# A pre-norm linear-attention and token-mixing block: the attention numerator computed for two token tiles at a time, with the order of the work around it rewritten

## The chip, the cores and the metric

The program runs on one core of a Trainium2 chip, in one launch, with all inputs and the output in the chip's main memory. The metric is device microseconds (us) of one execution, lower is better. Engines are named as the profile names them: PE (matrix multiplication), PEld (its weight loads), DVE (vector engine), ACT (activation engine), POOL (GpSimd) and SP (which only issues transfers here).

## The reference, cut to what matters

The input x has 2048 tokens and 512 channels. There are 32 heads of 16 channels, and the hidden width of the token mixer is 1792.

```python
def _A_ref(x, wqkv, w_phi, wo):
    q, k, v = heads(x @ wqkv)
    pq = jnp.einsum("bhsd,hdf->bhsf", q, w_phi)
    pk = jnp.einsum("bhsd,hdf->bhsf", k, w_phi)
    phi_q = jnp.concatenate([_softmax(pq), _softmax(-pq)], axis=-1)
    phi_k = jnp.concatenate([_softmax(pk), _softmax(-pk)], axis=-1)
    kv = jnp.einsum("bhsf,bhsd->bhfd", phi_k, v)
    z  = jnp.einsum("bhsf->bhf", phi_k)
    num = jnp.einsum("bhqf,bhfd->bhqd", phi_q, kv)
    den = jnp.einsum("bhqf,bhf->bhq", phi_q, z)[..., None] + 1e-6
    return merge(num / den) @ wo

def _B_ref(x, w1, b1, w2, b2):
    h = _layernorm(x)
    u = _gelu(jnp.einsum("bsd,sf->bdf", h, w1) + b1)
    return transpose(jnp.einsum("bdf,fs->bds", u, w2) + b2)

h = x + _A_ref(_layernorm(x), A_wqkv, A_w_phi, A_wo)
h2 = h + _B_ref(_layernorm(h), B_w1, B_b1, B_w2, B_b2)
```

Everything is float32. Two products that need float32 accuracy at speed are split: an operand is written as a high part and a low remainder in a shorter format (`F32R`), and three matmuls (high×high, high×low, low×high) take the place of one. `mm3` issues such a triple, `split` makes the two parts: ACT copies the high part, another engine subtracts it from the source.

## The kernel before

The tokens are cut into 16 tiles of 128. The program has four stages. First the weights are folded and k, v of all tiles are computed, which gives the summed matrix kv and the sums z. Six tiles' q logits are made in that stage too. The second stage, a loop `for it in range(NT + 3)`, is where the change lies: it finishes attention tile by tile, adds the residual, normalizes, and begins the token mixer. The third stage does the rest of the mixer's first matrix, the fourth its second matrix.

In the second stage a token tile t goes through these steps:

- `q_mm` (12 matmuls, PE) makes the q logits, `logit_ops` (three passes on DVE, from tile 6 on a fourth and fifth on POOL, in `negate`) subtracts the maximum and minimum, `exps` (ACT) takes the exponential into the tile `eq`, and `q_sum` (two reductions on DVE) makes the softmax sums.
- `s_ez` (POOL, line 442) multiplies `eq` with z; `s_den` (six small DVE operations) makes from it the weights `w` that hold both softmax sums and the denominator; `s_pq` (POOL, line 460) multiplies `eq` with `w`.
- `s_tr` transposes the eight blocks of `eq` on PE (line 525) into the PSUM tile `tn`, and ACT copies it to `pht` (line 527, two copies).
- `s_num` multiplies with kv: 16 small matmuls (line 543), each on 64 rows and 32 columns of the array, with 128 moving columns, into `tn` again. ACT copies the high part to `oh` (line 547), DVE the rest to `ol` (`s_ol`, line 552).
- `s_wo` (12 matmuls, PE) multiplies with the output weights into the PSUM tile `po`; `s_h` (DVE, line 568) adds x and sends the sum h to the output; SP issues that transfer.
- `s_moments` (ACT), `s_rstd` (two tiny POOL operations, lines 579 and 580) and `s_hn` normalize h: `hn` and the high part of `hs` on ACT (lines 584 and 57), the low part of `hs` on POOL (line 58).
- `fill(p)` then adds this tile's share to hidden column pair p of the mixer's first matrix (6 matmuls, PE). Its weights come by `fill_load`: a transfer on SP, the high part on ACT (line 604), the low part `wlo` on DVE (line 596), which is put off until `flush`.

The order on PE, DVE, ACT and POOL in this stage is the order of the program's text (`manual_schedule`); each engine works off its list strictly in order. Only SP's list, and all lists from the third stage on, are set by a planner. A tile's buffer is written again when its last reader is done: `tn` and `po` have one buffer, `pht`, `oh` and `ol` two, `h` four.

An iteration `it` works on different tiles at once: `s_num(it-1)`, `s_wo(it-2)`, `s_tr(it)`, `s_pq(it+1)`, `s_den(it+2)`, `s_ez(it+3)`, `s_moments`, `s_rstd` and `s_hn` of `it-3`, `fill(0)` for tile `it-4`, and, once all q logits are done, up to two steps of `fill(1)`. On PE an iteration is thus: 16 numerator matmuls, 12 for wo, 8 transposes, 12 for a q tile or two fills. On POOL it is: `s_pq`, `s_rstd`, `s_ez`, as long as there are any the two operations of `negate`, and the low part of `hs`.

Of the kernel before, what the change touches and what calls it, by code (L numbers as in the profile page):

```python
# [9 lines left out]
F32 = mybir.dt.float32  # L10
F32R = mybir.dt.float32r
# [13 lines left out]
Q_AT = (4, 6, 8, 9, 11, 13)  # L25
V_NOT = (0, 1, 11)
SUMS = 8
LAG = 4
WARM = 9
EPS = 1e-5  # L30

# [2 lines left out]
def block_kernel(ctx: ExitStack, tc: tile.TileContext, x, xT, wT, phic, wo, w1, b1, w2, b2,  # L34
# [25 lines left out]
    def mm3(o, ah, al, bh, bl, first, last):  # L60

        nc.tensor.matmul(o, ah, bh, start=first, stop=False)  # L62
        nc.tensor.matmul(o, ah, bl, start=False, stop=False)  # L63
        nc.tensor.matmul(o, al, bh, start=False, stop=last)  # L64
# [90 lines left out]
    def negate():  # L155

        if MN:
            ev, mx, mn = MN.pop(0)
            nc.gpsimd.tensor_sub(mn, mn, mx)
            nc.gpsimd.tensor_sub(ev[:, :, 1], mn.unsqueeze(3).to_broadcast([P, NPR, 2, DH]), ev[:, :, 0])  # L160

    def turns(*lists):

        return [ops[i] for i in range(max(map(len, lists))) for ops in lists if i < len(ops)]

    def run(*lists):
        for op in turns(*lists):
            op()
# [197 lines left out]
    def q_logits(lag):  # L366
        n = q["logits"]
        if n < min(NT, q["mm"] - lag + NT * (q["mm"] == NT)):
            EQ[n] = big.tile([P, NG, P], F32, name="eq", tag="big")
            q["logits"] += 1  # L370
            return logit_ops(PS[n], EQ[n], n >= len(Q_AT))
        return []
# [7 lines left out]
    def q_sums(lag):  # L380
        n = q["sum"]
        if n < min(NT, q["exp"] - lag + NT * (q["exp"] == NT)):
            q["sum"] += 1
            return q_sum(n)
        return []
# [54 lines left out]
    def s_ez(t):  # L440
        EZ[t] = az.tile([P, NG, P], F32, name="ez")
        nc.gpsimd.tensor_mul(EZ[t], EQ[t], zB)  # L442

    def s_den(t):


        tz = az.tile([P, NPR, 2, 2], F32, name="tz")
        den = az.tile([P, NPR, 2], F32, name="den")
        W[t] = az.tile([P, NPR, 2, 2], F32, name="w", bufs=3)
        other = SQ[t]  # L450
        return [lambda: nc.vector.reduce_sum(tz.rearrange("p g c h -> p (g c h)"), heads(EZ[t]), axis=AX.X),
                lambda: nc.vector.scalar_tensor_tensor(tz[:, :, 0], other[:, :, 1], 1e-6, tz[:, :, 0],
                                                       op0=ALU.mult, op1=ALU.add),
                lambda: nc.vector.tensor_mul(tz, other, tz),
                lambda: nc.vector.reduce_sum(den, tz.rearrange("p g c h -> p g h c"), axis=AX.X),
                lambda: nc.vector.reciprocal(den, den),
                lambda: nc.vector.tensor_mul(W[t], other, den.unsqueeze(2).to_broadcast([P, NPR, 2, 2]))]  # L457

    def s_pq(t):
        nc.gpsimd.tensor_mul(heads(EQ[t]), heads(EQ[t]), W[t].rearrange("p g c h -> p (g c h)").unsqueeze(2).to_broadcast([P, 2 * H, DH]))  # L460

    def lead(it, mm):

        if 0 <= it + 3 < NT:
            s_ez(it + 3)
        negate()
        for _ in range(mm):
            q_mm()
        q_exp(0)
# [49 lines left out]
    HN, HT, PHT, OS, PO, VE = {}, {}, {}, {}, {}, {}  # L519

    def s_tr(t):
        PHT[t] = ak.tile([P, NG, P], F32, name="pht")
        ptr = ps_t.tile([P, 2, 4, P], F32, name="tn")
        for g in range(NG):
            nc.tensor.transpose(ptr[:, g // 4, g % 4, :], EQ[t][:, g, :], ident)  # L525
        for half in range(2):
            nc.scalar.activation(PHT[t][:, half * 4:half * 4 + 4, :], ptr[:, half], AF.Copy)  # L527

    def s_kv():

        pt = ps_o.tile([P, 2, P], F32, name="po")
        for b in range(2):
            nc.tensor.transpose(pt[:, b, :], kvS[:, 2 * b:2 * b + 2, :].rearrange("p n f -> p (n f)"), ident)
        nc.scalar.activation(kvB, pt, AF.Copy)

    def s_num(t):

        pn = ps_t.tile([P, 2, 4, P], F32, name="tn")[:, :, 0:2]
        for b in range(2):
            for c in range(4):  # L540
                for r in range(2):
                    rows, cols = slice(64 * r, 64 * r + 64), slice(32 * c, 32 * c + 32)
                    nc.tensor.matmul(pn[cols, r, b, :], kvB[rows, b, cols], PHT[t][rows, 4 * b + c, :],  # L543
                                     start=True, stop=True, skip_group_check=True)
        oh = ak.tile([P, 2, 2, P], F32R, name="oh")
        ol = ak.tile([P, 2, 2, P], F32R, name="ol")
        nc.scalar.activation(oh, pn, AF.Copy)
        OS[t] = oh, ol, pn

    def s_ol(t):  # L550
        oh, ol, pn = OS[t]
        return [lambda: nc.vector.tensor_sub(ol, pn, oh)]

    def s_wo(t):
        oh, ol, _ = OS.pop(t)
        PO[t] = po = ps_o.tile([P, D], F32, name="po")
        for j in range(4):
            mm3(po, oh[:, j // 2, j % 2, :], ol[:, j // 2, j % 2, :], woh[:, j, :], wol[:, j, :], j == 0, j == 3)

    def s_x(t):  # L560
        HT[t] = ak.tile([P, D], F32, name="h", bufs=4)
        nc.sync.dma_start(HT[t], x[t * P:(t + 1) * P, :])

    def s_h(t):

        h = HT[t]
        VE[t] = ak.tile([P, 4], F32, name="ve2", bufs=3)
        nc.vector.scalar_tensor_tensor(h, PO.pop(t), 1.0, h, op0=ALU.mult, op1=ALU.add, accum_out=VE[t][:, 2:3])
        nc.sync.dma_start(out[t * P:(t + 1) * P, :], h)

    def s_moments(t):

        junk = ak.tile([P, D], F32, name="hj", bufs=1)
        nc.scalar.activation(VE[t][:, 1:2], VE[t][:, 2:3], AF.Copy, scale=-1.0 / D)
        nc.scalar.activation(junk, HT[t], AF.Square, bias=VE[t][:, 1:2], accum_out=VE[t][:, 3:4])
        nc.scalar.activation(VE[t][:, 0:1], VE[t][:, 3:4], AF.Identity, scale=(1.0 + EPS) / D, bias=eps2)
# [5 lines left out]
    def s_hn(t):  # L582
        hn = ak.tile([P, D], F32, name="hn")
        nc.scalar.activation(hn, HT[t], AF.Identity, scale=r2[:, t:t + 1], bias=VE[t][:, 1:2])
        HN[t] = big.tile([P, 2, D], F32R, name="hs", tag="big")
        split(HN[t][:, 0], HN[t][:, 1], hn, nc.gpsimd)
# [6 lines left out]
    def flush():  # L593
        while LATER:
            wl_, raw, wh_ = LATER.pop(0)
            LO.append(nc.vector.tensor_sub(wl_, raw, wh_).ins)  # L596
# [14 lines left out]
    def fill_load(p):  # L611
        if FL[p] < NT:
            WI[p, FL[p]] = stream(w1v, FL[p], 2, p * 256, 256)
            FL[p] += 2

    def fill(p, pool=None):

        t = FN[p]
        FN[p] = t + 1
        if FL[p] <= t:  # L620
            fill_load(p)
            flush()
        if t == 0:
            PU[p] = [pool.tile([P, D], F32, name="pu", tag="pu") for _ in range(2)]
        a, b = WI[p, t - t % 2]
        for c in range(2):
            mm3(PU[p][c], a[:, t % 2, c * P:(c + 1) * P], b[:, t % 2, c * P:(c + 1) * P],
                HN[t][:, 0], HN[t][:, 1], t == 0, t == NT - 1)

    for it in range(NT + 3):  # L630
        if 0 <= it < NT:
            s_x(it)
        if 0 <= it - 1 < NT:
            s_num(it - 1)
        if 0 <= it - 3 < NT:
            s_moments(it - 3)
        if 0 <= it - 2 < NT:
            s_wo(it - 2)
        if it == 1:
            run(q_logits(0))  # L640
            q_mm()
        if 0 <= it < NT:
            s_tr(it)
        if it == 0:
            s_kv()
        if 0 <= it + 1 < NT:
            s_pq(it + 1)
        if 0 <= it - 3 < NT:
            s_rstd(it - 3)
        lead(it, 1)  # L650
        den = s_den(it + 2) if it + 2 < NT else []
        ql = q_logits(1)
        ops = turns((s_ol(it - 1) if 0 <= it - 1 < NT else []) + ql + (q_sums(0) if it > 0 else []), den)

        at = 7 if ql else 3
        ops[at:at] = [flush]
        ops[3:3] = [lambda: s_h(it - 2)] if 0 <= it - 2 < NT else []
        run(ops)
        if it > 0:
            negate()  # L660
        if 0 <= it - 3 < NT:
            s_hn(it - 3)
        if FN[0] <= it - LAG:
            fill(0, ps_f)
        for _ in range(2):
            if q["logits"] == NT and FN[1] <= it - LAG:
                fill(1, ps_q)
        for p in range(2):
            if it >= LAG - 2 and FL[p] <= FN[p] + 1:
                fill_load(p)  # L670
    flush()
    ms.close()
# [197 lines left out]
```

## Time and profile before

| | us |
|---|---|
| median of 3 runs (532.62 to 533.29) | 532.62 |
| the profiled execution | 532.78 |
| its span in the profile | 531.0 |
| PE busy | 522.6 (98%) |
| DVE busy | 379.0 (71%) |
| ACT busy | 272.2 (51%) |
| POOL busy | 231.0 (44%) |
| granted PE clock | 1.00 |

The second stage lies from about 144 to 268 us of the span. A share of busy time is a mean over the whole span: POOL has little to do from 268 us on, and much before. The profile's list of the chain shows work that followed without a gap, so there the start of a piece to the start of the next is the time that it costs on the path; the duration of a single PE matmul in the other views is longer than that, since matmuls overlap. A releaser in a row (`<-`) is what ended an engine's idle time before it.

### The profile page before, as it was taken

What the parts mean: (1) busy time and instruction counts of PE and PEld (TensorE: products, weight loads), DVE (VectorE), ACT (ScalarE), POOL (GpSimd) and SP (SyncE); (2) the same over time, 40 slices, a digit from 0 to 9 for tenths busy, and PEclk for the clock granted to TensorE, in tenths of its full rate; (3) what the DMA queues carried; (4) which work ended last, traced back from release to release, by engine and by line L of the source; (5) the groups of instructions that cost most, each with busy time, mean ns of one, the idle gap of its engine ahead of it and who ended that gap; (6) DMA issues with size and microseconds to landing.
All of it is one profiled execution on the core that took longest, in us unless ns stands there. A gap on an engine that the chain in (4) does not pass through costs nothing.

```text
span 531.0 us, 9886 instructions
## 1 busy us (share of the span) xinstructions
PE 522.6 (98%) x3872; PEld 450.6 (85%) x3872; DVE 379.0 (71%) x680; ACT 272.2 (51%) x460; POOL 231.0 (44%) x190
## 2 busy tenths in 40 slices
PE   8999999999999999999999999999999999999995
PEld 7888888886877877777888888888899999999995
DVE  6993999877699888774426424735668878888874
ACT  6998833524237667766657323526444243343340
POOL 2589699877979988985335000000001101100110
PEclk9999999999999999999999999999999999999999
DMA  8633310012302233333255333542015556536641
GB/s 312 193 123 119 90 32 21 1 45 96 101 2 93 68 98 120 120 120 109 91 172 166 102 97 99 160 119 81 20 41 111 135 151 155 124 120 144 136 78 43
DMA packets 45487, 55.85 MB, mean 105 GB/s; under 512 B 3968, under 2 KB 33024, under 8 KB 45440
## 3 DMA queue, kind: packets, MB, share of 16 engines
q1 hardware_dynamic: 43136, 51.38, 31.0%
q0 software_dynamic: 2016, 3.67, 5.4%
q8 instruction: 30, 0.49, 0.4%
q10 hardware_dynamic: 288, 0.17, 0.1%
q14 instruction: 17, 0.14, 0.1%
HBM read 46.81 MB, written 8.39 MB: 104 GB/s over the span
## 4 chain that ended last, share of the span: by engine, by line
PE 93%; DVE 4%; ACT 1%; issue 1%; POOL 0%; DVEq 0%; ACTq 0%; POOLq 0%
PE py L764 26%; PE pu L62 12%; PE pu L64 12%; PE pu L63 12%; PE po L62 3%; PE po L63 3%; PE po L64 3%; PE tn L525 3%; PE pv L63 2%; PE pv L64 2%; PE pv L62 2%; PE pk_ps L62 2%; PE pk_ps L64 2%; PE pk_ps L63 2%; PE tn L543 2%; PE kvp L207 1%
## 5 line engine op out<-in xcount | busy, mean ns | idle before, releaser
L802 POOL DMA_DIRECT2D out<-ot x14 | 12.5, 999 | 211.7 <-DVE ot L800 211.7
L764 PE MATMUL py<-uf,whi 128*128 128x256 f32 x560 | 96.2, 283 | 0.0
L57 ACT ACTIVATE whi<-wraw 128x1792 fp32r<-128x1792 f32 x28 | 47.7, 1705 | 77.9 <-PE py L764 67.2
L62 PE MATMUL pu<-hs,whi 128*128 128x512 f32 x224 | 87.6, 394 | 0.0
L63 PE MATMUL pu<-hs,whi 128*128 128x512 f32 x224 | 87.3, 390 | 0.0
L64 PE MATMUL pu<-hs,wlo 128*128 128x512 f32 x224 | 87.1, 390 | 0.2 <-DVE wlo L596 0.2
L764 PEld LDWEIGHTS py<-uf,whi 128*128 128x128 f32 x560 | 83.3, 192 | 0.0
L596 DVE TENSOR_TENSOR wlo<-wraw,whi 128x512 fp32r<-128x512 f32 x56 | 45.1, 816 | 48.2 <-ACT whi L604 47.8
L764 PE MATMUL py<-uf,wlo 128*128 128x256 f32 x280 | 70.0, 283 | 0.0
L58 DVE TENSOR_TENSOR wlo<-wraw,whi 128x1792 fp32r<-128x1792 f32 x28 | 56.6, 2023 | 18.1 <-ACT whi L57 18.0
L604 ACT ACTIVATE whi<-wraw 128x512 fp32r<-128x512 f32 x56 | 34.4, 626 | 45.5 <-PE pu L63 41.4
L64 PEld LDWEIGHTS pu<-hs,wlo 128*128 128x128 f32 x224 | 42.1, 188 | 9.3 <-DVE wlo L596 0.6
L764 PEld LDWEIGHTS py<-uf,wlo 128*128 128x128 f32 x280 | 49.7, 192 | 0.0
L63 PEld LDWEIGHTS pu<-hs,whi 128*128 128x128 f32 x224 | 42.1, 188 | 8.4
L62 PEld LDWEIGHTS pu<-hs,whi 128*128 128x128 f32 x224 | 42.1, 188 | 8.4
L442 POOL TENSOR_TENSOR ez<-eq,zB 128x1024 f32<-128x1024 f32 x16 | 39.1, 2446 | 2.5 <-ACT zB L488 2.5
L764 PE MATMUL py<-un,whi 128*128 128x256 f32 x224 | 38.4, 283 | 0.0
L195 POOL TENSOR_TENSOR pk<-pk,sk 128x1024 f32<-128x1024 f32 x16 | 31.0, 1940 | 9.8 <-DVE sk L194 9.0
L527 ACT ACTIVATE pht<-tn 128x512 f32<-128x512 f32 x32 | 17.4, 595 | 34.5 <-PE tn L525 34.5
L460 POOL TENSOR_TENSOR eq<-eq,w 128x1024 f32<-128x1024 f32 x16 | 31.0, 1940 | 5.4 <-DVE w L457 5.4
L764 PEld LDWEIGHTS py<-un,whi 128*128 128x128 f32 x224 | 33.2, 192 | 0.1
L199 POOL TENSOR_TENSOR zacc<-zacc,pk 128x1024 f32<-128x1024 f32 x13 | 31.2, 2404 | 0.6
(165 smaller groups left out, 1187.6 us busy)
## 6 DMA issues: line engine op xcount, KB each, us to landing
wraw<-in_w SPq DMA_DIRECT2D x112, 256.0 KB, 3.0
xraw<-in_xT SPq DMA_DIRECT2D x16, 256.0 KB, 3.0
xh<-in_x SPq DMA_DIRECT2D x16, 256.0 KB, 2.6
h<-in_x SPq DMA_DIRECT2D x16, 256.0 KB, 3.6
out<-h SPq DMA_DIRECT2D x16, 256.0 KB, 2.0
out<-ot POOLq DMA_DIRECT2D x14, 256.0 KB, 4.4
wraw<-in_wT SPq DMA_DIRECT2D x12, 256.0 KB, 5.0
wo<-in_wo SPq DMA_DIRECT2D x4, 256.0 KB, 4.2
```

What stands on the lines that cost most here:

```text
L57: nc.scalar.activation(hi, src, AF.Copy)
L58: lo_engine.tensor_sub(lo, src, hi)
L62: nc.tensor.matmul(o, ah, bh, start=first, stop=False)
L63: nc.tensor.matmul(o, ah, bl, start=False, stop=False)
L64: nc.tensor.matmul(o, al, bh, start=False, stop=last)
L195: nc.gpsimd.tensor_mul(heads(PK[t]), heads(PK[t]), sk.unsqueeze(2).to_broadcast([P, 2 * H, DH]))
L199: nc.gpsimd.tensor_add(zacc, zacc, PK[t])
L442: nc.gpsimd.tensor_mul(EZ[t], EQ[t], zB)
L460: nc.gpsimd.tensor_mul(heads(EQ[t]), heads(EQ[t]), W[t].rearrange("p g c h -> p (g c h)").unsqueeze(2).to_broadcast([P, 2 * H, DH]))
L596: LO.append(nc.vector.tensor_sub(wl_, raw, wh_).ins)
L604: nc.scalar.activation(wh_, raw, AF.Copy)
L764: nc.tensor.matmul(o, a[x], b[:, y], start=start and i == 0, stop=stop and i == 2, skip_group_check=True)
```

## The change

`s_num` takes a pair of token tiles: `pht` holds both tiles' transposes side by side, and each of the 16 small matmuls has 256 moving columns, filling all of `tn`. It is called in even iterations only, so there are 8 calls in place of 16. `oh` and `ol` hold a pair, still made by one ACT copy and one DVE subtraction for each token tile. `pht`, `oh` and `ol` now have one buffer, of twice the size.

The loop's body has a new order. On PE an even iteration is: numerator of the pair, the q tile's 12 matmuls or the fills, wo, transposes; an odd one: q tile or fills, transposes, wo. `fills` puts both fills in one place, `fill(0)` for tile `it-5` (`LAG` is 5) and `fill(1)` one tile behind it. On DVE the subtractions `ol` of the pair come first, with the first step of `s_den` between them, and `s_h` comes last, behind `flush`. On POOL an even iteration is now `s_pq(it+1)`, low part of `hs` for tile it−4, `s_ez(it+3)`, `s_rstd(it-3)`, low part of `hs` for tile it−3; an odd one is `s_pq`, `s_ez`, `s_rstd`, with `negate`'s operations behind as before. On ACT an even iteration is: the two copies `oh`, `s_hn(it-4)`, the exponential, `s_moments(it-3)`, the copies of `pht`, `s_hn(it-3)`, the weights' high part; an odd one: the exponential, copies of `pht`, `s_moments(it-3)`, the weights' high part. `fill` flushes only if its own weights are still waiting, and `fill_load` runs by a new condition.

```diff
-LAG = 4
+LAG = 5
...
     def s_tr(t):
-        PHT[t] = ak.tile([P, NG, P], F32, name="pht")
+        j, i = divmod(t, 2)
+        if i == 0:
+            PHT[j] = ak.tile([P, NG, 2, P], F32, name="pht", bufs=1)
...
-    def s_num(t):
-
-        pn = ps_t.tile([P, 2, 4, P], F32, name="tn")[:, :, 0:2]
+    def s_num(j):
+
+
+        pn = ps_t.tile([P, 2, 4, P], F32, name="tn")
...
-                    nc.tensor.matmul(pn[cols, r, b, :], kvB[rows, b, cols], PHT[t][rows, 4 * b + c, :],
+                    nc.tensor.matmul(pn[cols, r, 2 * b:2 * b + 2, :], kvB[rows, b, cols], PHT[j][rows, 4 * b + c, :, :],
...
+        oh = ak.tile([P, 2, 2, 2, P], F32R, name="oh", bufs=1)
+        ol = ak.tile([P, 2, 2, 2, P], F32R, name="ol", bufs=1)
+        pv = pn.rearrange("p r (b i) s -> p i r b s", i=2)
+        for i in range(2):
+            nc.scalar.activation(oh[:, i], pv[:, i], AF.Copy)
...
+    def fills(it):
+        if FN[0] <= it - LAG:
+            fill(0, ps_f)
+        if FN[1] < it - LAG:
+            fill(1, ps_q)
+
     for it in range(NT + 3):
...
+        even = it % 2 == 0
+        if 0 <= it + 1 < NT:
+            s_pq(it + 1)
...
+        if it > 1 and even:
+            if it <= NT:
+                s_num(it // 2 - 1)
+            if it >= 4:
+                s_hn(it - 4)
+        den = s_den(it + 2) if it + 2 < NT else []
+        if it > 1 and even and it <= NT:
+            ol = s_ol(it // 2 - 1)
+            run(ol[:1] + den[:1] + ol[1:])
+            den = den[1:]
+        if it < NT:
+            s_x(it)
+        if it + 3 < NT:
+            s_ez(it + 3)
+        negate()
+        q_mm()
+        fills(it)
+        q_exp(0)
+        logits = q_logits(1)
+        if it >= 3 and even:
+            s_moments(it - 3)
+        if it > 1 and even and it - 2 < NT:
+            s_wo(it - 2)
+        if 1 < it < NT:
+            s_tr(it)
+        if it > 1 and not even and it - 2 < NT:
+            s_wo(it - 2)
+        if it >= 3 and not even:
+            s_moments(it - 3)
+        if it >= 3:
+            s_rstd(it - 3)
+        run(logits + (q_sums(0) if it > 0 else []), den)
+        flush()
+        if 0 <= it - 2 < NT:
+            s_h(it - 2)
+        if it > 0:
+            negate()
+        if it >= 3 and even:
+            s_hn(it - 3)
         for p in range(2):
-            if it >= LAG - 2 and FL[p] <= FN[p] + 1:
+            if it >= LAG - 3 + p and FL[p] <= FN[p] + 2 * (FN[p] > 0):
                 fill_load(p)
```

More of the change, by code (lines that the diff above doesn't have):

```diff
@@ L526, in s_tr @@
         for half in range(2):
-            nc.scalar.activation(PHT[t][:, half * 4:half * 4 + 4, :], ptr[:, half], AF.Copy)
+            nc.scalar.activation(PHT[j][:, half * 4:half * 4 + 4, i, :], ptr[:, half], AF.Copy)
     def s_kv():
@@ L542, in s_num, with s_ol @@
                     rows, cols = slice(64 * r, 64 * r + 64), slice(32 * c, 32 * c + 32)
-                    nc.tensor.matmul(pn[cols, r, b, :], kvB[rows, b, cols], PHT[t][rows, 4 * b + c, :],
+                    nc.tensor.matmul(pn[cols, r, 2 * b:2 * b + 2, :], kvB[rows, b, cols], PHT[j][rows, 4 * b + c, :, :],
                                      start=True, stop=True, skip_group_check=True)
[L545 to L552, printed above, removed]
+        oh = ak.tile([P, 2, 2, 2, P], F32R, name="oh", bufs=1)
[3 more added lines that the diff above has]
+            nc.scalar.activation(oh[:, i], pv[:, i], AF.Copy)
+        OS[j] = oh, ol, pv
+    def s_ol(j):
+        oh, ol, pv = OS[j]
+        return [lambda i=i: nc.vector.tensor_sub(ol[:, i], pv[:, i], oh[:, i]) for i in range(2)]
     def s_wo(t):
-        oh, ol, _ = OS.pop(t)
+        oh, ol, _ = OS[t // 2]
+        i = t % 2
         PO[t] = po = ps_o.tile([P, D], F32, name="po")
         for j in range(4):
-            mm3(po, oh[:, j // 2, j % 2, :], ol[:, j // 2, j % 2, :], woh[:, j, :], wol[:, j, :], j == 0, j == 3)
+            mm3(po, oh[:, i, j // 2, j % 2, :], ol[:, i, j // 2, j % 2, :], woh[:, j, :], wol[:, j, :], j == 0, j == 3)
     def s_x(t):
@@ L621, in fill @@
             fill_load(p)
+        if any(part is WI[p, t - t % 2][1] for part, _, _ in LATER):
             flush()
@@ L628, in fill @@
                 HN[t][:, 0], HN[t][:, 1], t == 0, t == NT - 1)
-    for it in range(NT + 3):
[L631 to L638, printed above, removed]
+    def fills(it):
[3 more added lines that the diff above has]
+            fill(1, ps_q)
+    for it in range(NT + 3):
+        even = it % 2 == 0
+        if 0 <= it + 1 < NT:
+            s_pq(it + 1)
+        if it == 0:
+            s_tr(0)
+            s_kv()
         if it == 1:
@@ L641, in block_kernel @@
             q_mm()
-        if 0 <= it < NT:
-            s_tr(it)
[L644 to L648, printed above, removed]
-            s_rstd(it - 3)
[L650 to L658, printed above, removed]
+            s_tr(1)
+        if it > 1 and even:
[22 more added lines that the diff above has]
+        if 1 < it < NT:
+            s_tr(it)
+        if it > 1 and not even and it - 2 < NT:
[3 more added lines that the diff above has]
+        if it >= 3:
+            s_rstd(it - 3)
+        run(logits + (q_sums(0) if it > 0 else []), den)
+        flush()
+        if 0 <= it - 2 < NT:
+            s_h(it - 2)
         if it > 0:
             negate()
-        if 0 <= it - 3 < NT:
+        if it >= 3 and even:
             s_hn(it - 3)
[L663 to L667, printed above, removed]
         for p in range(2):
-            if it >= LAG - 2 and FL[p] <= FN[p] + 1:
+            if it >= LAG - 3 + p and FL[p] <= FN[p] + 2 * (FN[p] > 0):
                 fill_load(p)
```

## The prediction

> **What bounds the kernel now.** I read the page's busy line first, then the chain, then the second stage by iterations.
>
> ```profile
> PE 522.6 (98%) x3872; PEld 450.6 (85%) x3872; DVE 379.0 (71%) x680; ACT 272.2 (51%) x460; POOL 231.0 (44%) x190
> ...
> POOL 2589699877979988985335000000001101100110
> ```
>
> PE is busy 98% of the span and so is the bound, but POOL's mean of 44% hides a stretch: slices 11 to 18, which hold most of the second stage, are at 8 or 9 tenths. One row per iteration (columns: stretch, length, busy time of PE, PEld, DVE, ACT, POOL, then clock, DMA share, GB/s) shows how near POOL is there.
>
> ```profile
> 181.38:189.00 7.62, 7.62 (x68) 6.10 (x66) 6.38 (x15) 5.78 (x11) 7.46 (x7) 1.00 0.34 105
> 189.00:197.56 8.56, 8.35 (x70) 6.27 (x70) 7.28 (x13) 6.18 (x12) 6.32 (x7) 1.00 0.27 92
> ...
> 211.97:219.13 7.16, 7.16 (x67) 5.67 (x65) 6.05 (x14) 4.21 (x9) 7.08 (x6) 1.00 0.46 149
> ```
>
> An iteration takes 7.16 us, all of it PE, and POOL is busy for 7.08 of them. So PE sets the pace, with POOL a hair behind. The chain of waits has these pieces of an iteration (start, length on the path, what), and the stage's one visible stall:
>
> ```profile
> 177.84 0.60 PE tn L543 x32
> ...
> 190.70 2.06 DVE wlo L596
> 192.80 0.50 PE pu L64
> ...
> 211.97 0.88 PE tn L525 x8
> 215.58 0.60 PE tn L543 x32
> 216.18 0.43 PE po L62
> 216.61 0.23 PE po L63
> ...
> 219.13 0.87 PE tn L525 x8
> ```
>
> The rows 181.38 to 197.56 hold two iterations (14.32) and one fill more (6 matmuls at 0.23, 1.38): 15.70 against 16.18, so that stall costs 0.5.
>
> **The numerator itself.** A burst of 16 small matmuls (32 records, two passes each) costs 0.60 until the next matmul starts, and that one 0.43 instead of 0.23, so 0.20 for changing over. What would 256 columns cost?
>
> ```profile
> L543 PE MATMUL tn<-pht,kvB 64*32 64x128 f32 x512 | 10.7, 275 | 0.0
> L207 PE MATMUL kvp<-pk,vs 128*32 128x64 f32 x512 | 9.1, 221 | 0.0
> ```
>
> 64 columns more lengthen a record by 54 ns, 0.84 ns a column. Eight places of the array (2 row halves, 4 column strips) work side by side, so 32 records are 4 in a row: 4 × 128 × 0.84 = 0.43 us, and 0.17 to fill and drain. A pair's burst is then 4 × 256 × 0.84 + 0.17 = 1.03, against 2 × 0.60, and changes over once: 0.17 + 0.20 = 0.37 saved a pair, eight pairs 3.0. Ends: 0.60 a burst if only the number of records counted (0.80 a pair, 6.4), and nothing saved (0). I take 3.0, since it follows from two rows.
>
> The Trainium skill, "TensorE: Matmul & The Clock Gate", section "Wait — 56ns, not 53.3ns?", says that matmuls never start closer than about 25 ns. By it 32 records would need 0.80 us, a pair would save 0.57 + 0.20, and eight pairs 6.2, 3.2 more. The trace has 32 records in 0.60, 19 ns each, so I don't use the rule.
>
> PE needs 2 × 7.16 − 0.37 = 13.95 a pair of iterations if nothing waits.
>
> **What moves at no cost.**
>
> ```profile
> L547 ACT ACTIVATE oh<-tn 128x512 fp32r<-128x512 f32 x16 | 9.5, 596 | 7.2 <-PE tn L543 7.2
> L552 DVE TENSOR_TENSOR ol<-tn,oh 128x512 fp32r<-128x512 f32 x16 | 11.0, 689 | 23.1 <-ACT oh L547 23.1
> ...
> wraw<-in_w SPq DMA_DIRECT2D x112, 256.0 KB, 3.0
> h<-in_x SPq DMA_DIRECT2D x16, 256.0 KB, 3.6
> ```
>
> ACT and DVE have as many `oh`, `ol` and `pht` operations as before. After a burst ACT and DVE need 0.60 + 0.69 until the first `ol` is there, while a q tile or fills (12 × 0.23 = 2.8) now lie between; without them wo would wait 1.5. The transposes wait for the second `ol`, another 2.8 later. `h` at DVE's end is wanted by the next wo (one `po` buffer), over 2 us on. SP has the same transfers (x in, h out, one weight block an iteration), which land in 3.0 to 3.6 us within a 7 us iteration. With fills later, one more is left after the last wo (7 for 6); PE's work is the same. Tile 15's `hs` must then be ready: h, moments, rstd, hn, hs and two weight copies are about 7 us by my estimate, and 44 matmuls (10 us) stand before its first use. All 0, at most 1 at that end.
>
> **POOL's ring.** Here I find the price. POOL's list in one iteration, from start to start:
>
> ```profile
> 162.74 1.94 POOL L460 TENSOR_TENSOR eq<-eq,w 128x1024 f32<-128x1024 f32 x1
> ...
> 176.47 0.25 POOL L159 TENSOR_TENSOR mn<-mn,mx 128x32 f32<-128x32 f32 x1
> 176.80 1.06 POOL L160 TENSOR_TENSOR eq<-mn,eq 128x512 f32<-128x512 f32 x1
> 177.82 1.28 POOL L58 TENSOR_TENSOR hs<-hn,hs 128x512 fp32r<-128x512 f32 x1
> ...
> 203.92 1.94 POOL L460 TENSOR_TENSOR eq<-eq,w 128x1024 f32<-128x1024 f32 x1 [0.59 <-DVE w L457]
> 205.82 0.55 POOL L579 TENSOR_TENSOR r<-ve,mhalf 128x1 f32<-128x1 f32 x1
> 206.45 0.19 POOL L580 TENSOR_TENSOR ve<-ve,r 128x1 f32<-128x1 f32 x1
> 206.59 2.40 POOL L442 TENSOR_TENSOR ez<-eq,zB 128x1024 f32<-128x1024 f32 x1
> 208.95 1.29 POOL L58 TENSOR_TENSOR hs<-hn,hs 128x512 fp32r<-128x512 f32 x1
> 210.20 1.93 POOL L460 TENSOR_TENSOR eq<-eq,w 128x1024 f32<-128x1024 f32 x1
> ```
>
> So pq 1.90, rstd 0.77, ez 2.36, hs 1.25 (and negate 1.35 while q logits are made): 6.28 an iteration, 12.56 a pair. In the order before, ez stands between rstd and hs and covers the normalizing on ACT. In the even iteration after, hs of tile it−3 follows its rstd directly. That wait, and the two ACT jobs behind it, look like this where POOL had nothing else to do:
>
> ```profile
> 261.78 0.19 POOL L580 TENSOR_TENSOR ve<-ve,r 128x1 f32<-128x1 f32 x1
> 262.00 0.82 ACT L584 ACTIVATE hn<-h,ve,r 128x512 f32<-128x512 f32 x1 [0.93 <-POOL ve L580]
> 262.85 0.63 ACT L57 ACTIVATE hs<-hn 128x512 fp32r<-128x512 f32 x1
> 263.56 1.29 POOL L58 TENSOR_TENSOR hs<-hn,hs 128x512 fp32r<-128x512 f32 x1 [1.59 <-ACT hs L57]
> ...
> 255.81 1.08 ACT L527 ACTIVATE pht<-tn 128x512 f32<-128x512 f32 x2 [1.89 <-PE tn L525]
> 263.39 1.14 ACT L604 ACTIVATE whi<-wraw 128x512 fp32r<-128x512 f32 x2
> ```
>
> POOL idles 1.6: 14.2 a pair. And POOL and DVE shut each other out when DVE subtracts `wlo`:
>
> ```profile
> 198.29 2.41 POOL L442 TENSOR_TENSOR ez<-eq,zB 128x1024 f32<-128x1024 f32 x1
> 198.78 3.07 DVE L596 TENSOR_TENSOR wlo<-wraw,whi 128x512 fp32r<-128x512 f32 x2
> ...
> 212.72 0.72 POOL L580 TENSOR_TENSOR ve<-ve,r 128x1 f32<-128x1 f32 x1
> 213.39 2.85 POOL L442 TENSOR_TENSOR ez<-eq,zB 128x1024 f32<-128x1024 f32 x1
> ...
> 212.69 1.29 DVE L596 TENSOR_TENSOR wlo<-wraw,whi 128x512 fp32r<-128x512 f32 x2
> ```
>
> Two wlo that meet an ez last 3.07 in place of 1.29, ending 0.6 a piece after it; two that come first lengthen ve and ez by 0.53 and 0.45. So 0.5 of POOL's time for each, two a pair. By DVE's new order the even one is issued just behind its w, while POOL is in ez, the odd one while POOL is in pq; neither falls into the 1.6 of idling. The ring rstd, ACT's hn and hs, POOL's hs, pq, ez, rstd, pq, hs, ez, rstd is then 14.2 + 1.0 = 15.2, 1.25 above PE's 13.95. PE feels it because ACT copies the odd tile's `pht` behind that hn and hs, and the next numerator waits for the copies.
>
> The Trainium skill, "SBUF — State Buffer", section "Who interferes with whom", says that a DVE operation with two SBUF inputs and a GpSimd operation that reads SBUF exclude each other for the whole instruction; by the full wlo (0.60) the ring would be 15.4 and the sum below 0.6 higher. The rows above give 0.5.
>
> **When it begins and ends.** pq of tile 4 starts at 162.74 in the trace before, set by DVE, which has much the same list in front of it after. From there POOL must do, up to the ez of tile 9: 4 pq (7.6), 4 ez (9.4), 3 rstd (2.3), 3 negate (4.1), 3 hs (3.8), two wlo (0.9) and about 1 of waits: 29.1, until 191.8. Then rstd 0.8 and the hand-over 1.6, hs at 194.2; ACT's two weight copies (1.1) and the copies of `pht` (1.1) let the pair numerator of iteration 8 start at 196.4. PE without waits: the burst at 177.84 has the same work behind it as two PE pieces (transposes 0.87, wo 2.75) before iteration 6's burst, less two pairs' saving: 177.84 + 3.6 − 0.7 = 180.7, plus 13.95 = 194.7. So POOL is late by 1.7 when it counts first. Three rounds follow (iterations 8, 10, 12; from 13 on there is no ez), 3 × 1.25 = 3.75; one weight copy fewer stands before the later numerators, −0.55. Together 4.9 of new stalls.
>
> **The sum.** −3.0 (numerator) − 0.5 (the old stall, in a place that PE now waits in anyway) + 4.9 = +1.4. Against the profiled execution, 532.78, that is 534.2; this run lies 0.16 above the median of the runs shown, so against the median it is 534.0.
>
> **The rivals.**
>
> 1. PE keeps its pace: the wlo fall into POOL's idle time or exclude nothing. The ring is 14.2, new stalls are 1.7 − 0.9 at the entry, 3 × 0.25, less 0.55: 1.0 at most and 0 at best, so −2.5 to −3.5, 529.1 to 530.1. It decides as soon as the ring is under about 14.3. For it: the PE row shows no stall at all in most iterations, with POOL at 7.08 of 7.16. Against it: POOL's idle 1.6 is one ninth of the ring, so few wlo can fall there by chance.
> 2. One wlo of two is lost on POOL: ring 14.7, 3 × 0.75 + 1.3 − 0.55 = 3.0 of stalls, −0.5: 532.1. Also about the time if the burst of 256 columns were as short as the old one, since its 3.4 would be lost on POOL in three or four pairs of eight.
> 3. The new burst saves nothing (1.20 + 0.20 for a pair, as if columns went at half the rate assumed for the second tile): the ring hides it in some four pairs, the others lose 4 × 0.37: +2.9, 535.5.
>
> **How the numbers follow.** A difference under 0.2% (1.07 us) is about what a measurement of this kernel can't tell from none. Forecast 0.50 (534.0, its own range 533.7 to 535.3), rival 1 0.25, rival 2 0.16, rival 3 0.09. Faster is rival 1, same is rival 2, slower the other two: 0.25, 0.16, 0.59. The range leaves out the lower part of rival 1 and reaches past rival 3: 529.9 to 535.7.
>
> **What would show it.** Right: `tn` L543 rows of 1.0 us in the chain, x32, eight times; pairs of iterations of 15.2 between about 181 and 241 us and 13.95 behind; PE idle before them for ACT's `pht`; POOL idle about 1.6 before an L58 once a pair; ACT's hn waiting for ve. Wrong: pairs of 14 throughout (rival 1), wlo of 0.69 with ez of 2.4 throughout, or a burst far from 1.03. What would break the forecast is above all a stall of POOL or DVE that the queue lists don't show, or an entry with more slack than the 0 that I count at iteration 7.

## The result, and the profile after

The changed kernel takes 534.89 us in the median (534.41 to 535.27), the kernel before in runs beside it 533.07 (532.62 to 533.86): a ratio of 1.0034, 95% interval 1.0023 to 1.0045, or 1.8 us slower. The prediction was 534.0, slower, and the time lies in its range. The profiled execution took 534.41 with a span of 532.6, so its span is 1.6 us longer than before.

Two lines of the page: the busy times, and the shares of the chain by engine.

```profile
PE 520.8 (98%) x3616; PEld 448.7 (84%) x3616; DVE 384.4 (72%) x680; ACT 271.9 (51%) x460; POOL 234.8 (44%) x190
...
PE 83%; POOL 9%; DVE 3%; ACT 2%; issue 1%; DVEq 0%; POOLq 0%; ACTq 0%
```

PE's busy time is 1.8 us shorter and the span 1.6 us longer, so PE is idle for 3.4 us more. PE loses more than that: the pairs of iterations below hold the same matmuls, and yet PE counts as busy for 13.95 to 14.48 us of them, because a matmul lasts 0.39 us in the timeline while the next one starts 0.23 behind it, so that part of each wait counts as busy. The waits are therefore read from the starts of the numerators. POOL, which had no share of the chain before that the page shows as more than 0%, now holds 9% of it. POOL has 3.8 us and DVE 5.4 us more of busy time with as many instructions as before (190 and 680): their instructions got longer.

One row per pair of iterations, cut at the starts of the numerators (stretch, length, busy time of PE, PEld, DVE, ACT, POOL, then clock, DMA share, GB/s):

```profile
180.86:197.34 16.48, 14.48 (x96) 11.01 (x96) 14.71 (x31) 11.33 (x23) 14.65 (x13) 1.00 0.29 88
197.34:211.36 14.02, 13.95 (x96) 11.09 (x96) 12.68 (x23) 9.44 (x22) 12.27 (x11) 1.00 0.40 118
211.36:226.44 15.08, 14.44 (x97) 11.07 (x96) 13.61 (x25) 9.26 (x21) 13.33 (x11) 1.00 0.34 105
226.44:241.53 15.09, 14.31 (x96) 11.06 (x96) 11.78 (x23) 9.28 (x21) 13.34 (x11) 1.00 0.39 119
241.53:255.55 14.02, 14.02 (x104) 11.16 (x112) 5.71 (x9) 10.88 (x25) 8.73 (x9) 1.00 0.40 125
```

The pace without waits is in the chain, from 154.17 to 168.08: 13.91. The five rows are 74.69 for 5 × 13.91 = 69.55, so 5.1 of new waits, half of it in the first row. The chain through the rounds in between (start, length on the path, what):

```profile
154.17 1.02 PE tn L546 x32
...
168.08 1.02 PE tn L546 x32
...
192.82 0.83 ACT hn L590
193.68 0.64 ACT hs L57
194.38 1.29 POOL hs L58
195.68 2.34 POOL eq L460
198.02 2.81 POOL ez L442
200.83 0.51 POOL r L585
201.60 1.89 POOL eq L460
203.50 1.24 POOL hs L58
204.74 2.35 POOL ez L442
207.09 0.96 POOL r L585
208.35 0.83 ACT hn L590
209.20 0.64 ACT hs L57
209.91 1.29 POOL hs L58
...
239.99 0.52 ACT whi L610
240.51 0.97 ACT pht L529 x2
241.53 1.10 PE tn L546 x32
```

This is the ring that the prediction describes, step by step in its order: rstd, ACT's two jobs, hs, pq (L460), ez (L442), rstd, pq, hs, ez, rstd. The path leaves it only at 239.99, through ACT's weight copy and the copies of `pht`, into the numerator. The instructions themselves, from the timeline of POOL and DVE (start, length, what; in brackets idle time and what ended it):

```profile
209.91 1.29 POOL L58 TENSOR_TENSOR hs<-hn,hs 128x512 fp32r<-128x512 f32 x1 [1.59 <-ACT hs L57]
211.87 1.77 DVE L602 TENSOR_TENSOR wlo<-wraw,whi 128x512 fp32r<-128x512 f32 x1
213.05 2.87 POOL L442 TENSOR_TENSOR ez<-eq,zB 128x1024 f32<-128x1024 f32 x1
...
220.40 2.32 DVE L602 TENSOR_TENSOR wlo<-wraw,whi 128x512 fp32r<-128x512 f32 x1
222.12 1.01 POOL L585 TENSOR_TENSOR r<-ve,mhalf 128x1 f32<-128x1 f32 x1
...
225.00 1.30 POOL L58 TENSOR_TENSOR hs<-hn,hs 128x512 fp32r<-128x512 f32 x1 [1.59 <-ACT hs L57]
```

From one hs behind POOL's wait to the next is 15.09 us (209.91 to 225.00). Two wlo lie in it. The first waits for pq and then holds up ez (2.87 where 2.40 is usual), the second waits for ez and then holds up a tiny operation on 128 × 1 elements (1.01 where 0.55 is usual).

### The profile page after: what moved, and what is told of

Read it like the earlier page. It is cut to its first block, busy times and chain, and to the rows that moved or that the text cites. A ratio compares the mean times of both kernels' runs of the same rounds, so it can differ in the third digit from the quotient of the medians.

```text
span 532.6 us, 9386 instructions
## 1 busy us (share of the span) xinstructions
PE 520.8 (98%) x3616; PEld 448.7 (84%) x3616; DVE 384.4 (72%) x680; ACT 271.9 (51%) x460; POOL 234.8 (44%) x190
## 4 chain that ended last, share of the span: by engine, by line
PE 83%; POOL 9%; DVE 3%; ACT 2%; issue 1%; DVEq 0%; POOLq 0%; ACTq 0%
PE py L789 26%; PE pu L62 11%; PE pu L63 11%; PE pu L64 11%; POOL ez L442 4%; POOL eq L460 3%; PE pv L63 2%; PE pv L64 2%; PE pv L62 2%; PE pk_ps L62 2%; PE pk_ps L63 2%; PE pk_ps L64 2%; POOL hs L58 2%; PE po L62 1%; PE kvp L207 1%; PE po L63 1%
## 5 line engine op out<-in xcount | busy, mean ns | idle before, releaser
L602 DVE TENSOR_TENSOR wlo<-wraw,whi 128x512 fp32r<-128x512 f32 x56 | 50.3, 903 | 51.8 <-ACT whi L610 50.7
L58 DVE TENSOR_TENSOR wlo<-wraw,whi 128x1792 fp32r<-128x1792 f32 x28 | 56.6, 2022 | 15.4 <-ACT whi L57 15.4
L442 POOL TENSOR_TENSOR ez<-eq,zB 128x1024 f32<-128x1024 f32 x16 | 40.9, 2559 | 2.5 <-ACT zB L488 2.5
L460 POOL TENSOR_TENSOR eq<-eq,w 128x1024 f32<-128x1024 f32 x16 | 32.0, 1997 | 4.0 <-DVE w L457 4.0
L58 POOL TENSOR_TENSOR hs<-hn,hs 128x512 fp32r<-128x512 f32 x16 | 21.4, 1340 | 17.5 <-ACT hs L57 15.6
```

What stands on the lines that cost most here:

```text
L58: lo_engine.tensor_sub(lo, src, hi)
```

## The experiments

In all of them the times are medians, with the lowest and the highest behind, and the kernel before ran beside each of them at 532.85 to 533.12. (VectorE in the expectations is DVE.) Three theories are at stake: POOL's ring sets the slow pairs (the prediction); DVE's order sets them, since wlo, h and the denominators were moved there too; or the numerator saves less than reckoned.

**1. ez behind rstd.** The same work, but in even iterations from 6 on POOL's ez stands behind rstd, so that it covers ACT's normalizing.

```diff
-        if it + 3 < NT:
+        late = even and it >= 6
+        if it + 3 < NT and not late:
             s_ez(it + 3)
...
             s_rstd(it - 3)
+        if it + 3 < NT and late:
+            s_ez(it + 3)
```

> The changed kernel, with ez moved behind rstd on POOL in the even iterations from 6 on, so that it covers the hand-over POOL to ACT to POOL again. Ring theory: hs of tile it-3 no longer idles POOL for 1.6, the ring is 12.6 + 1.0 of exclusion = 13.6, under PE's 13.95, so most of the 4.9 us of stalls go: pairs of iterations at about 14.0 from iteration 8 on, time 530.8 to 531.8. Rival (POOL's total load with the wlo exclusions is the bound, the idle 1.6 is only slack that shows up there): the pairs stay at 15.1, time 534.9. Rival (the stall comes from DVE's or ACT's new order): no change either, with the waits at the same places.

Measured 531.63 (531.19 to 532.03), ratio 0.9972 (0.9961 to 0.9984). One instruction of POOL in an iteration, moved behind rstd, turns a slower kernel into a faster one than before. Pairs of this kernel:

```profile
180.82:195.93 15.11, 14.48 (x105) 11.09 (x112) 12.57 (x30) 12.28 (x26) 14.88 (x14) 1.00 0.31 93
195.93:210.62 14.69, 14.22 (x104) 10.99 (x111) 14.31 (x27) 10.10 (x22) 13.43 (x11) 1.00 0.41 126
210.62:224.53 13.91, 13.91 (x104) 11.07 (x111) 13.53 (x24) 9.49 (x21) 12.87 (x11) 1.00 0.35 114
```

The later rounds run at PE's 13.91. Two pairs at the entry keep 2.0 of waits.

**2. wlo without two SBUF operands.** SBUF is the memory that holds the tiles, PSUM the one that PE's sums go to. In the stage's loop the subtraction takes its second operand from a PSUM tile with other data (`sums`); the weights' low parts are wrong in this kernel, and the work is as much as before.

```diff
-            LO.append(nc.vector.tensor_sub(wl_, raw, wh_).ins)
+            other = sums.rearrange("p s g c h -> p (s g c h)").rearrange("p (k w) -> p k w", k=2) if IN_LOOP else wh_
+            LO.append(nc.vector.tensor_sub(wl_, raw, other).ins)
```

> The changed kernel, where the wlo subtraction inside the loop takes its second operand from PSUM (the softmax sums) in place of the high part; so the mixer's low parts of the blocks loaded there are wrong. As many DVE operations of about the same length, with one operand in SBUF in place of two. Ring theory: no exclusion, POOL's ez, pq, r at their 2.40, 1.94, 0.55 everywhere, wlo at 0.69; the ten lengthened POOL operations between 168 and 241 us give back 4.5 us, of which up to 4 on the path: ring 14.2, pairs 14.0 to 14.3, time 530.9 to 531.8. Rival (exclusion costs DVE only, or falls into idle time): 534.5 to 534.9.

Measured 531.79 (531.17 to 532.32), ratio 0.9976 (0.9966 to 0.9986). Two of POOL's hs behind its wait:

```profile
208.96 1.29 POOL L58 TENSOR_TENSOR hs<-hn,hs 128x512 fp32r<-128x512 f32 x1 [1.59 <-ACT hs L57]
...
223.12 1.29 POOL L58 TENSOR_TENSOR hs<-hn,hs 128x512 fp32r<-128x512 f32 x1 [1.59 <-ACT hs L57]
```

The ring is 14.16 with the order of the changed kernel and its idle 1.59, the 14.2 that the prediction had without wlo. So two wlo cost the ring 0.93, 0.46 each. The Trainium skill, "SBUF — State Buffer", section "Who interferes with whom", says that such a subtraction and a POOL instruction that reads SBUF shut each other out; the longer ez and r of the changed kernel, gone in this one, agree.

**3. Without the ez products.** Both kernels without the ez product from tile 8 on; the denominator's sum is taken over zB itself, so the denominators of these tiles are not those of the reference. This takes 2.4 us an iteration off POOL, and what is left of the difference between the two kernels is not POOL's.

```diff
+        if t >= 8:
+            EZ[t] = zB
+            return
```

> The changed kernel without the ez product from tile 8 on; the denominator's first step reduces zB in its place (so the denominators of these tiles are wrong). DVE's list is the same, POOL has 2.4 us less per iteration. Ring theory: POOL is off the path, no stall is left, 4.9 us less: 530.0, and pairs of 13.95 throughout. It gives the numerator's own price against the same edit of the kernel before: -3.0 by the count of columns, -6.4 if only the number of matmuls counted, 0 if nothing is saved. Rival (the stall comes from the order on ACT or DVE): stays near 534.9.

> The same edit in the kernel before: PE is the bound there, so all theories expect almost nothing: 532.5 to 533.1, at most the one stall of 0.5 gone.

Measured 530.37 (530.20 to 530.78) for the changed kernel and 532.49 (531.99 to 532.91) for the kernel before. With POOL out of the way the change gains 2.1, not 3.0. The pair at the entry of the changed one shows what is missing:

```profile
180.94:195.81 14.87, 14.23 (x105) 11.01 (x112) 13.73 (x31) 12.87 (x27) 10.02 (x12) 1.00 0.29 98
```

The pairs behind it take 13.91, so this one waits 0.96; the chain shows it as PE waiting for a wlo on DVE at 188.89. That is the kind of wait that the kernel before had at 190.70.

**4. One POOL operation more in the ring.** POOL's subtraction for hs, 1.25 us, done twice for tiles 5, 7 and 9.

```diff
         split(HN[t][:, 0], HN[t][:, 1], hn, nc.gpsimd)
+        if t in (5, 7, 9):
+            nc.gpsimd.tensor_sub(HN[t][:, 1], hn, HN[t][:, 0])
```

> The changed kernel with POOL's subtraction for hs (1.25 us) done twice for tiles 5, 7 and 9, in the iterations 8, 10 and 12 whose rounds are said to be POOL's ring. If the ring sets these rounds, each is longer by 1.25: +3.75, 538.2 to 538.9 (+2.5, 537.4, if the entry hides the first). If PE or VectorE sets the pace and POOL only waits beside it: 534.5 to 535.5.

Measured 537.72 (537.38 to 538.51), 2.8 more than the changed kernel. POOL's hs behind its wait come at

```profile
210.01 1.29 POOL L58 TENSOR_TENSOR hs<-hn,hs 128x512 fp32r<-128x512 f32 x1 [1.59 <-ACT hs L57]
...
226.42 1.30 POOL L58 TENSOR_TENSOR hs<-hn,hs 128x512 fp32r<-128x512 f32 x1 [1.59 <-ACT hs L57]
...
242.81 1.30 POOL L58 TENSOR_TENSOR hs<-hn,hs 128x512 fp32r<-128x512 f32 x1 [1.59 <-ACT hs L57]
```

so rounds of 16.41 and 16.39 in place of 15.09: 1.3 each for 1.25 put in, 2.6 in two rounds. The third stands behind the last ez, and no round follows it; the expectation of 3.75 counted a third round that isn't there. Experiments 1 to 4 each touch the ring in another way, and PE follows each time; that the ring sets these rounds is shown.

**5. What the numerator's saving consists of.** On experiment 1, where PE sets most pairs, the pair's numerator is taken with 128 columns at a time. In the first form the two tiles stand side by side, so that two matmuls in a row go to the same place of the array:

```diff
-                    nc.tensor.matmul(pn[cols, r, 2 * b:2 * b + 2, :], kvB[rows, b, cols], PHT[j][rows, 4 * b + c, :, :],
...
+                    for i in range(2):
+                        nc.tensor.matmul(pn[cols, r, 2 * b + i, :], kvB[rows, b, cols], PHT[j][rows, 4 * b + c, i, :],
...
```

> The kernel of e1_ez_behind_rstd (531.63, where PE sets most pairs again), but each weight slice of the numerator multiplies 128 columns twice in place of 256 once: 64 records a pair, one changeover, the same columns. What the saving of a pair consists of is asked. If a record's columns set the burst (0.84 ns a column, four records in a row, as in the prediction), nothing changes: burst 1.0 to 1.1, time 531.4 to 532.0. If the number of records counts (0.60 for 32), the burst is 1.2 and eight pairs cost 1.4 more, of which the two pairs at the entry may hide some: 532.7 to 533.1. If 256 columns in one record were what saved time beyond that, more still.

Measured 533.63 (533.26 to 534.18): 2.0 more than experiment 1. The burst is longer than the 1.0 to 1.1 and the 1.2 expected by columns and by records, as the chain shows (the start of each burst, its length):

```profile
225.61 1.41 PE tn L547 x64
...
239.91 1.40 PE tn L547 x64
```

In the second form the loop over `i` is the outermost, so that the first tile's 16 matmuls stand ahead of the second's (cut; the lines below the new loop move in by one step):

```diff
+        for i in range(2):
             for b in range(2):
                 for c in range(4):
                     for r in range(2):
-                        nc.tensor.matmul(pn[cols, r, 2 * b:2 * b + 2, :], ...
+                        nc.tensor.matmul(pn[cols, r, 2 * b + i, :], ...
```

> The kernel of e1_ez_behind_rstd with the pair's numerator as two bursts of 128 columns back to back, the first tile's 16 matmuls and then the second's, each in the order before. In e5_ez_behind_rstd_two_bursts both tiles' matmuls stood side by side, so that two in a row went to the same place of the array; the pair's burst was 1.40 against 1.02 and nothing of the saving was left. If places that are filled twice in a row made that, the burst is now 1.03 (by columns: 8 x 128 x 0.84 ns + 0.17), and the time that of e1, 531.3 to 532.0. If a burst of 32 records costs 0.60 whatever stands behind it, 1.20 a pair, 532.4 to 533.0. If it is the number of records or the 256 columns, 1.40 again: 533.2 to 534.0.

Measured 531.83 (531.54 to 533.57), as experiment 1 (531.63) to within their spread.

```profile
224.65 1.09 PE tn L547 x64
...
238.64 1.09 PE tn L547 x64
```

Pairs are 13.99 here, 13.91 with 256 columns, 14.30 in the first form, and 14.3 (twice 7.16) before. So of the 0.4 that a pair saves, 0.3 comes from one burst for two tiles, with one start, one end and one changeover, and 0.08 from the 256 columns. It is not the number of records: 64 of them take 1.09, 17 ns each. The Trainium skill's figure of about 25 ns between the starts of two matmuls ("TensorE: Matmul & The Clock Gate", section "Wait — 56ns, not 53.3ns?"), which the prediction set aside, is contradicted by this row too. The Trainium skill, "TensorEngine Tiling (Array Packing)", section "Key Properties", says that a change of the tiling mode drains the matrix engine; that one changeover in place of two saves time agrees. Why two in a row at one place cost 0.3 a pair was not tried further.

**6. h ahead of the sums.** One step of DVE's new order, moved back alone in the changed kernel.

```diff
+        if 0 <= it - 2 < NT:
+            s_h(it - 2)
         run(logits + (q_sums(0) if it > 0 else []), den)
         flush()
-        if 0 <= it - 2 < NT:
-            s_h(it - 2)
```

> The changed kernel, with h ahead of the sums, the denominator and the wlo on VectorE, as far as the order before had it early. The ring theory has h at no cost on VectorE's end, since the ring runs rstd, ACT's hn and hs, POOL's hs, pq, ez and none of these waits for h: 534.4 to 535.4, as after (534.89). If the late h is what makes hn late (moments and rstd wait for it), h first gains: 532 to 534. If VectorE then waits for PE's wo with the sums behind it, it loses: 535.5 to 537.

Measured 554.11 (552.57 to 554.35), 19 us slower than the changed kernel and far outside all three expectations. Three rows of its timeline tell why:

```profile
214.46 0.80 PE L64 MATMUL pu<-hs,wlo 128*128 128x512 f32 x1 [4.43 <-DVE wlo L602]
...
221.12 0.69 DVE L574 SCALAR_TENSOR_TENSOR h<-po,h 128x512 f32<-128x512 f32 x1 [4.39 <-PE po L64]
...
222.00 1.09 ACT L529 ACTIVATE pht<-tn 128x512 f32<-128x512 f32 x2 [10.18 <-PE tn L527]
```

h waits for wo, and wo now comes late in PE's list. Behind h on DVE stand the sums, `w` and wlo, and PE's fills wait for the wlo: PE and DVE wait for each other in turn. With wo this late on PE, h has to stand behind them.

**7. Fills one tile later, alone.** The kernel before with `LAG` 5.

```diff
-LAG = 4
+LAG = 5
```

> The kernel before with every fill one tile later (LAG 5 in place of 4), the one part of the change that can be had alone. The prediction had it at 0, at most 1 at the end of the stage: the same work of PE, two tiles' fills moved behind the last wo. Expected 532.5 to 533.6 against 533.02. If the fills one tile later also take away the stall of 0.5 where a fill waited for its wlo, 532.3 to 532.7; if the last tile's hs is late, up to 534.

Measured 535.81 (535.04 to 535.89), 2.7 more than before, which I had not expected. Two iterations of it:

```profile
178.00:185.66 7.66, 6.88 (x40) 4.94 (x46) 7.62 (x19) 5.25 (x12) 7.56 (x7) 1.00 0.43 138
...
207.13:215.97 8.84, 7.35 (x72) 5.58 (x79) 8.53 (x18) 4.48 (x10) 6.14 (x6) 1.00 0.37 119
```

The change moves 12 matmuls (2 × 1.36) from the middle of the stage to behind its end. The middle hardly gets shorter: DVE and POOL are busy for nearly all of the first row, DVE for the second, and PE waits 0.8 and 1.5 where it had worked. From the third numerator to the sixteenth are 95.96 us here (162.94 to 258.90) and 96.33 in the kernel before (162.17 to 258.50): 0.4 less for 2.7 us of work taken out. The work had filled time in which PE would wait.

**8. The second pair's lag undone.** `FN[1] <= it - LAG` for `<`, in the changed kernel (first) and in that of experiment 9 (second).

> The changed kernel with only the second pair's lag undone. The entry waits 2.5 in after, set by POOL's ring, and the ring doesn't ask when PE has its fills: the fill goes into waiting time and its 1.36 is gone from the tail: 533.2 to 534.0 against 534.89. If a fill a tile earlier waits for hs and its weights on PE with the transposes behind it, nothing gained or a loss: 534.7 to 536.5. The prediction had this part at 0.

> The kernel of e6_early_wlo (530.94), with the second pair's fills no longer a tile behind the first's: one fill (1.36 of PE) comes ahead of the entry instead of behind the last wo. In e8_before_lag5 the reverse move cost 2.7 for two fills, because they had filled time in which PE else waits. In e6 the pair of the entry is 15.26 for 14.24 of PE, so 1.0 of waiting is there to fill: 529.6 to 530.5 if that waiting is set by POOL and ACT as now. If the wait is for the wlo or hs of that very fill, it only moves: 530.6 to 531.6.

Measured 536.43 (535.94 to 537.97) and 535.09 (533.33 to 536.03): 1.5 and 4.2 slower than without it. The first is a loss that had been held possible, but for another reason; the second is above all that was expected. PE in the first of the two, at the first fill of the second pair, and then a window that begins there:

```profile
181.81 0.77 PE L62 MATMUL pu<-hs,whi 128*128 128x512 f32 x1 [3.23 <-DVE tz L454]
```

```profile
181.80:187.70 5.90, 5.89 (x18) 4.94 (x19) 1.90 (x5) 2.46 (x7) 3.02 (x3) 0.51 0.05 19
```

This pair's sums go into the two buffers that hold q logits, and PE waits 3.2 us for DVE to be done with the last of these. In the kernel before a condition on the q logits kept this from happening; in the changed kernel the lag does it. The row with 0.51 is the granted clock behind that wait; the last section comes back to it.

**9. wlo earlier at the entry.** Experiment 1, with `flush` ahead of the sums and denominators in iterations 6 to 8.

```diff
+        if 6 <= it <= 8:
+            flush()
         run(logits + (q_sums(0) if it > 0 else []), den)
         flush()
```

> The kernel of e1_ez_behind_rstd, and in iterations 6 to 8 VectorE's wlo are issued ahead of the sums and the denominator instead of behind them. In e1's trace two pairs are still long, 15.11 and 14.69 where 13.91 is the pace, and both times PE waits for a wlo on VectorE (at 188.8 and 198.7), so this is the old stall of the kernel before in a new place. If VectorE's order is the cause, 0.6 to 1.6 of these 2.0 go: 530.0 to 531.0. If POOL's ring is still what ends last there, or VectorE then waits for ACT's whi instead, nothing is gained: 531.4 to 532.2.

Measured 530.94 (530.62 to 531.63), ratio 0.9962 (0.9948 to 0.9976), the fastest of all kernels here that compute the whole reference, 0.7 under experiment 1. The two ratios' intervals overlap, so the times alone don't show this gain; the pairs of the two profiles do, 29.17 for two against 29.80:

```profile
181.54:196.80 15.26, 14.24 (x105) 11.09 (x111) 14.08 (x25) 12.45 (x26) 15.03 (x13) 1.00 0.36 115
196.80:210.71 13.91, 13.91 (x104) 11.12 (x111) 12.99 (x31) 9.95 (x22) 13.75 (x12) 1.00 0.37 114
```

The second long pair is gone (14.69 to 13.91), the first is not: there PE now waits for an hs on POOL (188.59), which has 15.03 to do in 15.26.

## Why the prediction was right, by its own steps

- **The numerator, −3.0.** Right. A pair takes 13.91 where two iterations took 14.3, eight times 0.4 is 3.2. The burst is 1.02 where 1.03 was worked out from the columns' rate and 0.17 for start and end. Experiment 5 bears out the parts too: 0.3 of the 0.4 is saved by one burst in place of two, 0.08 by the 256 columns in one record. That makes rival 3 wrong, and the end of 6.4 from counting records.
- **The old stall, −0.5.** Right in the sum, because PE waits for POOL in that place anyway, but the stall is not gone. With POOL lightened (experiment 3) the entry still waits 0.96 for a wlo on DVE, and in experiment 1 part of 2.0.
- **POOL's ring, 15.2.** Right: 15.09 and 15.07 from hs to hs, 1.59 of it idle, 14.16 without the exclusion. Each wlo costs 0.46 for 0.5, so the 15.4 by a wlo's full length isn't reached. (The reading of the page before is loose in one place: of the slices 11 to 18 of POOL, slice 12 is at 7 tenths. Nothing hangs on it.) The prediction's reason that neither falls into the 1.6 of idling holds in the rows shown. Where PE feels the ring is only in part as predicted. The numerator at 197.41 waits 1.43 for `pht`, but in the second and the third round most of the wait comes earlier, at the fill that needs POOL's hs (this row, and 0.61 at 234.95); the numerators at 226.44 and 241.53 then start 0.2 to 0.3 late, as soon as `pht` is copied:

```profile
219.87 0.50 PE L63 MATMUL pu<-hs,whi 128*128 128x512 f32 x1 [0.62 <-POOL hs L58]
```

- **The entry, 1.7.** Mis-sized: the first row of pairs has 16.48 for 13.91, 2.6. POOL's hs was put at 194.2 and comes at 194.38, but the numerator was put at 196.4 and comes at 197.41. Between ACT's weight copies and its copies of `pht` stands the last exponential of the q tiles, which was left out:

```profile
194.21 1.14 ACT L610 ACTIVATE whi<-wraw 128x512 fp32r<-128x512 f32 x2
...
195.26 1.14 ACT L171 ACTIVATE eq<-eq,r 128x1024 f32<-128x1024 f32 x1
...
196.30 1.06 ACT L529 ACTIVATE pht<-tn 128x512 f32<-128x512 f32 x2
...
197.41 1.10 PE L546 MATMUL tn<-pht,kvB 64*32 64x256 f32 x32 [1.43 <-ACT pht L529]
```

- **Three rounds of 1.25.** Mis-sized by the same thing, the other way. POOL's first round is 15.53 (a double wlo lengthens pq and ez in it, and a third r), but the next numerator has neither this exponential (1.04 from start to start) nor the second weight copy (0.53) ahead of it: 13.96 by these numbers, 14.02 in the row. The second and third rounds cost 1.2 each. What the first numerator loses to the exponential the next one gets back, so it cancels in the total, and that isn't luck. Entry and rounds together were put at 4.9 and are 5.1.
- **The sum.** −3.2 − 0.6 (the stalls of before) + 5.1 = +1.3, where the spans differ by 1.6 and the medians by 1.8. Some 0.2 of the rest is the late h, as the next point shows.
- **What moves at no cost.** h last on DVE was put at 0 and costs 0.2 once. The pair from 168.08 to 180.86 has one fill less (1.36) than the 13.91 of the others and takes 12.78 for 12.55. In it PE's weight load for wo waits for the h that frees `po`, and the first wo matmul, at 177.92 in the chain, takes 0.43 for 0.23:

```profile
177.84 0.19 PEld L62 LDWEIGHTS po<-woh,oh 128*128 128x128 f32 x1 [0.17 <-DVE h L574]
```

Nor is it a free choice, since h first costs 19 us with this order of PE. Behind the last numerator (255.55) PE waits for nothing, so the stage's end costs 0, as forecast. The fills were wrong as a rule: "PE's work is the same" is true, and yet moving two of them out of the stage costs the kernel before 2.7. In the sum this did no harm, for there the fill that the entry misses lies under POOL's lateness. How much of the 5.1 the later fills are responsible for stays open: the second pair can't go earlier (experiment 8), and the first pair's fill a tile earlier was not tried in the changed kernel, where hs of an even tile is made in that very iteration.
- **The rivals.** Rival 1 needed wlo that exclude nothing; experiment 2 makes that true, and the kernel is then at 531.79, not 529.1 to 530.1, because the entry's waits don't go away with it. Rival 2 needed one wlo of two to be free, and both cost.

## What to carry to other kernels

An engine with a mean of 44% can be the bound of a stage: write down its list over one round, with the time that it must idle for a hand-over, and compare that with the bounding engine's round. If the two are near each other, a cheap thing to try is an independent long instruction between the one that others wait for and the one that waits for them, as ez between rstd and hs here: worth 3.3 us without any work removed.

Work that one can put anywhere on the bounding engine isn't free to move. It belongs where that engine would else wait; moving it to an end where the engine is never idle cost nearly its full time in experiment 7.

## What was not expected of the hardware

After PE's wait of 3.23 us in the first kernel of experiment 8 the granted clock was 0.51 for 5.9 us, and matmuls started 0.43 us apart in place of 0.23; experiment 6 has the same 0.43 behind its wait of 4.43. At half the clock, 5.9 us are some 3 us lost on top of the wait.

But the length of one wait doesn't settle it. The second kernel of experiment 8 waits the same 3.23 us, until 180.95, in its profiled execution and keeps its clock:

```profile
180.95:186.85 5.90, 5.90 (x57) 4.39 (x58) 2.60 (x7) 3.56 (x9) 4.41 (x6) 1.00 0.04 13
```

That execution took 533.39 with a mean granted clock of 0.999. Four of the other five took 535.01 to 536.03, with 0.991 to 0.996. So about 2.4 of the 4.2 that this kernel lost come without a lower clock, and the rest came with it. And in the profiled execution of experiment 4 the clock was 0.50 from 238 to 240 us, where PE had waited only 1.12 and 0.65 a little before; at 538.51 it is the longest of its four. The changed kernel's own waits, 1.43 at most among those shown, show a clock of 1.00 in every row above. What decides was not tried further.

The Trainium skill, "TensorE: Matmul & The Clock Gate", section "Part 1: The HAM clock gate (the "warmup" mystery)", tells of half the clock after an idle window of about 3.4 us and of the full clock after about 3.4 us of work. The wait of 4.43 agrees with the first; the waits of 3.23, 1.12 and 0.65 that half the clock followed are shorter. The second is exceeded by the 5.9 measured here.

Small matmuls at eight places of the array pay for their order: 64 of them took 1.09 us when neighbours went to different places, and 1.40 when two in a row went to the same.
